# A fused attention and gated-MLP kernel: the U half of w_in by the hardware queue with casts on the engines, and w_spatial and two thirds of batch 1's q transposed by DMA

## The chip, the cores and the metric

One Trainium2 chip, one core. Times are device microseconds of a whole execution. The kernel before took 247.88 us, the median of three runs (247.47, 247.88, 248.72). The profiled execution is the one that took 247.47.

## The reference

Eight batches. Attention with 16 query heads that share 4 key and value heads, over 384 positions of 64 elements, then a gated MLP whose gate mixes positions:

```
k, v repeated 4 times over the heads                 # q: 8 x 16 x 384 x 64; k, v: 8 x 4 x 384 x 64
attn = softmax(q @ k.T / sqrt(64)) @ v
x = attn with the heads side by side                 # 8 x 384 x 1024
h = relu(x @ w_in); u, v = halves of h               # w_in 1024 x 1024, halves of 512
v_n = (v - mean) / sqrt(var + 1e-6)
v_s = w_spatial @ v_n (over positions) + b_spatial   # 384 x 384
out = (u * v_s) @ w_out                              # 512 x 1024
```

Inputs and outputs are fp32. The kernel multiplies in fp16 and sums in fp32.

## The kernel before

All five engines run an order that is written out. Three strings, FIRST (batches 0 to 2 and the weights), STEADY (run for batches 3 to 6) and LAST (batch 7), list steps such as `S,0` or `cq,1,0,0,3,1,0,1,p`; the function `run` calls the function behind each name, and `tc.manual_schedule` keeps that order on every engine and on SP's DMA queue. A step's first number is a batch, relative to the string's; a last letter v, s or p puts a copy or cast on VectorE, ScalarE or GpSimd. An engine takes its own steps strictly in order, so whatever stands behind a step that waits is held too.

The steps that matter here:

- **Loads.** `lk`, `lq`, `lv` load k, q, v of a batch as fp32 by SP's hardware queue (one first q load by ScalarE's). Their fp32 tiles have one buffer, so a batch's load waits for the casts of the batch before. `lwi,0,part,g` (line 249) loads a quarter of one half of w_in by GpSimd's software queue, which casts to fp16 on the way: part 1 is the V half, part 0 the U half, four DMAs each. `lws`, `lbi`, `lwo` load w_spatial, the bias and w_out; w_out comes in four fp32 pieces of 128 rows through two buffers, and `cwo` casts them.
- **Casts and transposes.** `ck`, `cq`, `cv` cast to fp16. For batches 0 and 1 `Tk` and `Tq` transpose on TensorE against an identity (lines 334 and 349), one q tile of four blocks at a time, and `tk`, `tq` copy the PSUM result to SBUF. From batch 2 on, `dk` and `dq` (lines 308 and 317) do it with one DMA transpose each on SP's queue. w_spatial is cast by GpSimd (`cws`, line 274), transposed in nine blocks on TensorE (`Tw`, line 284) and copied by VectorE (`tw`, line 288).
- **Attention.** `S` is one score unit: a pair of matmuls (line 368) into one of two PSUM tiles; a batch has 18, three for each of two head groups and three q tiles. `E` is its exp on ScalarE (line 381), the larger part of ScalarE's work. `X` (line 395) is a third of one q tile's value product; part 2 of it sums the exps. `rl` and `re` make the reciprocal on ScalarE, `rv` on VectorE (line 416, batch 0's first tile only); `xm` multiplies and writes x.
- **MLP.** `V` makes v (line 438), `ru` its relu, `bs`, `rs`, `nm` the normalisation. `G` is a pair of half-array products side by side: `gs` (with w_spatial), `gu` (with the U half of w_in), `go` (with w_out), and `w12`, `w24`, `w10`, which pair `V` of one batch with the output product of another. `mk` is a small write that orders the two phases of a pair. `sa`, `gt` add the bias and gate; `oc` and `st` copy and store the output. LAST uses the unpaired forms `SP`, `U`, `O`.
- **Warm.** `W` are matmuls on the identity that fill TensorE's early waits.

PSUM has two double tiles for scores and four banks that every other product takes in turn; a bank is free again after its last reader.

Of the kernel before, what the change touches and what calls it, by code (L numbers as in the profile page):

```python
# [21 lines left out]
W,0,1 W,0,4 lk,0,0,2 lq,0,0,0,1,0,1,s lq,0,1,0,1 W,0,4 W,0,2 W,0,2 W,0,2 W,0,3 W,0,4 lk,0,2,4  # L22
cq,0,0,0,1,0,0,1,s lq,0,0,1,3 lq,0,1,1,3 lk,1 lv,0 lv,1 lq,1,0 lq,1,1 ck,0,0,0,3,p Tk,0,0,0,3 W,0,4
W,0,4 tk,0,0,0,3,v cq,0,0,0,1,1,0,1,v Tq,0,0,0,0,1 tq,0,0,0,0,1,v W,0,4 ck,0,1,0,3,p
cq,0,1,0,1,1,0,1,p cq,0,1,0,1,0,0,1,p S,0 lk,2 E,0 lws,0 S,0 Tk,0,1,0,3 W,0,4 W,0,2 lq,2,0 lbi,0
Tq,0,1,0,0,1 S,0 lwi,0,1,1 lwi,0,1,2 lwi,0,1,3 cq,0,0,1,3,0,0,1,p tq,0,1,0,0,1,v tk,0,1,0,3,v
cq,0,1,1,3,1,0,1,p cq,0,0,1,3,1,0,1,v W,0,2 E,0 W,0,1 S,0 lq,2,1 E,0 S,0 Tq,0,0,1,0,1 W,0,1 W,0,2
S,0 cq,0,1,1,3,0,0,1,v tq,0,0,1,0,1,v Tq,0,1,1,0,1 S,0 W,0,4 ck,1,1,0,3,p ck,1,0,0,3,p lwi,0,1,0
cv,0,p S,0 W,0,1 Tq,0,1,2,0,1 Tk,1,0,0,3 tk,1,0,0,3,v tq,0,1,1,0,1,v tq,0,1,2,0,1,v Tq,0,0,2,0,1
tq,0,0,2,0,1,v E,0 E,0 E,0 E,0 E,0 S,0 X,0,0,2 S,0 S,0 X,0,0,0 E,0 S,0 rv,0,0 X,0,0,1 xm,0,0,0 E,0  # L30
E,0 S,0 E,0 X,0,1,2 E,0 S,0 xm,0,0,1 X,0,1,1 X,0,1,0 S,0 rl,0,1 E,0 re,0,1 cq,1,0,0,1,0,0,1,p E,0
S,0 Tk,1,1,0,3 V,0,0,0,4 V,0,0,4,8 lwi,0,0,3 S,0 S,0 cq,1,1,1,3,1,0,1,p lwi,0,0,0 lwi,0,0,2 cv,1,v
xm,0,1,1 xm,0,1,0 E,0 ck,2,1,0,3,p cq,1,1,1,3,0,0,1,p cws,0,0 lwi,0,0,1 cq,1,0,1,3,1,0,1,v cws,0,2
cws,0,1 ck,2,0,0,3,p cq,1,0,0,1,1,0,1,s tk,1,1,0,3,v E,0 Tq,1,0,0,0,1 V,0,1,0,4 tq,1,0,0,0,1,v
ru,0,0,v cq,1,0,1,3,0,0,1,v cq,1,1,0,1,0,0,1,v E,0 cq,1,1,0,1,1,0,1,v S,0 X,0,2,2 V,0,1,4,8
Tq,1,1,0,0,1 ru,0,1,v S,0 tq,1,1,0,0,1,v E,0 rl,0,2 S,0 X,0,2,0 re,0,2 E,0 E,0 X,0,2,1 xm,0,2,0
xm,0,2,1 S,0 E,0 Tq,1,0,1,0,1 Tq,1,1,1,0,1 V,0,2,0,4 S,0 S,0 cq,2,0,0,3,1,0,1,p cq,2,0,0,3,0,0,1,p
cq,2,1,0,3,1,0,1,p cq,2,1,0,3,0,0,1,p E,0 E,0 Tw,0,0,2 bs,0,0 tq,1,0,1,0,1,v bs,0,1 tw,0,0,2
tq,1,1,1,0,1,v Tq,1,0,2,0,1 V,0,2,4,8 X,1,0,2 S,0 S,0 ru,0,2,s X,1,0,0 rl,1,0 tq,1,0,2,0,1,v bs,0,2
X,1,0,1 lwo,0,1 dk,2 dq,2,0 lwo,0,0 Tw,0,2,3 Tq,1,1,2,0,1 re,1,0 xm,1,0,0 xm,1,0,1 S,0 E,0 rs,0  # L40
V,1,0,0,4 E,0 tq,1,1,2,0,1,v E,0 nm,0,0 V,1,0,4,8 dq,2,1 tw,0,2,3 nm,0,1 S,0 lwo,0,3 nm,0,2 ru,1,0,v
G,0,gs,2,0,0,1 S,0 lwo,0,2 mk,0,gs,2,v G,0,gs,0,0,0,1 G,0,gs,2,1,0,1 S,0 mk,0,gs,0,v E,0 E,0 E,0
sa,0,2 G,0,gs,0,1,0,1 S,0 sa,0,1 sa,0,0 sa,0,3 bs,1,0 X,1,1,2 E,0 cwo,0,1,1,p rl,1,1 X,1,1,0 X,1,1,1
S,0 cwo,0,0,0,p G,0,gu,2,0,0 S,0 re,1,1 xm,1,1,1 xm,1,1,0 G,0,gu,2,0,1 S,0 cwo,0,0,1,p G,0,gu,0,0,0
E,0 S,0 G,0,gu,0,0,1 mk,0,gu,2,v G,0,gu,2,1,0 lv,2 cwo,0,1,0,v S,0 lq,3,1 lk,3 lq,3,0 mk,0,gu,0,v
E,0 E,0 E,0 G,0,gu,2,1,1 S,0 G,0,gu,0,1,0 S,0 G,0,gu,0,1,1 E,0 S,0 cwo,0,3,1,p cwo,0,2,0,p gt,0,2
gt,0,0 gt,0,1 gt,0,3 cwo,0,3,0,v E,0 cwo,0,2,1,v X,1,2,2 X,1,2,1 S,0 S,0 E,0 E,0 rl,1,2 V,1,1,0,4
re,1,2 E,0 E,0 V,1,1,4,8 S,0 G,0,go,0,0,0 G,0,go,0,0,1 S,0 xm,1,2,1 ru,1,1,v cv,2,p mk,0,go,0,p
X,1,2,0 bs,1,1 xm,1,2,0 E,0 E,0 S,0 G,0,go,0,1,0 S,0 G,0,go,0,1,1 X,2,0,2 X,2,0,0 S,0 E,0 E,0
oc,0,0,v oc,0,1,s rl,2,0 E,0 G,1,w12,2,0,0 re,2,0 G,1,w12,2,0,1 ck,3,0,0,3,s S,0 cq,3,1,0,3,1,0,1,p  # L50
cq,3,1,0,3,0,0,1,p cq,3,0,0,3,1,0,1,p S,0 cq,3,0,0,3,0,0,1,p mk,1,w12,2,v ck,3,1,0,3,v xm,2,0,0 E,0
G,1,w12,2,1,0 G,1,w12,2,1,1 E,0 ru,1,2,s S,0 E,0 dk,3 lk,4 dq,3,0 lv,3 dq,3,1 oc,0,3,v oc,0,2,v S,0
X,2,1,2 rl,2,1 re,2,1 bs,1,2 X,2,0,1 X,2,1,1 E,0 X,2,1,0 S,0 xm,2,0,1 xm,2,1,1 G,2,w24,0,0,0
G,2,w24,0,0,1 S,0 S,0 rs,1 E,0 xm,2,1,0 mk,2,w24,0,v nm,1,0 nm,1,2 nm,1,1 G,2,w24,0,1,0 oc,0,4,v
G,2,w24,0,1,1 E,0 oc,0,5,v E,0 ru,2,0,s S,0 G,1,gs,0,0,0,1 E,0 S,0 mk,1,gs,0,v G,1,gs,0,1,0,1
G,1,gs,2,0,0,1 sa,1,0 mk,1,gs,2,v sa,1,1 S,0 G,1,gs,2,1,0,1 S,0 G,1,gu,0,0,0 sa,1,2 sa,1,3 E,0
G,1,gu,0,0,1 mk,1,gu,0,v S,0 G,1,gu,2,0,0 S,0 G,1,gu,2,0,1 G,1,gu,0,1,0 mk,1,gu,2,v S,0 G,1,gu,2,1,0
G,1,gu,0,1,1 S,0 G,1,gu,2,1,1 E,0 E,0 gt,1,0 gt,1,1 gt,1,2 gt,1,3 E,0 S,0 X,2,2,2 E,0 X,2,2,0 E,0
E,0 rl,2,2 E,0 re,2,2 G,2,w10,1,0,0 G,2,w10,1,0,1 S,0 S,0 mk,2,w10,1,v xm,2,2,0 G,2,w10,1,1,0
oc,1,0,v G,2,w10,1,1,1 S,0 X,2,2,1 oc,1,1,v E,0 E,0 lv,4 st,0,2 lq,4,0 st,0,0 ru,2,1,s cv,3,p bs,2,0  # L60
xm,2,2,1 E,0 lq,4,1 st,1,0 bs,2,1 st,0,1
# [3 lines left out]
cq,1,1,0,3,0,0,1,p X,0,0,2 lk,2 ck,1,1,0,3,p cq,1,1,0,3,1,0,1,p ck,1,0,0,3,p X,0,0,0 S,0 rl,0,0  # L65
G,-1,w12,2,0,0 G,-1,w12,2,0,1 mk,-1,w12,2,v cq,1,0,0,3,1,0,1,p S,0 S,0 re,0,0 E,0 G,-1,w12,2,1,0
G,-1,w12,2,1,1 E,0 xm,0,0,0 cq,1,0,0,3,0,0,1,v oc,-2,2,v S,0 X,0,1,2 dq,1,0 dk,1 lq,2,0 dq,1,1
ru,-1,2,s rl,0,1 oc,-2,3,v re,0,1 X,0,0,1 X,0,1,0 X,0,1,1 bs,-1,2 xm,0,0,1 xm,0,1,0 rs,-1 E,0
G,0,w24,0,0,0 G,0,w24,0,0,1 S,0 S,0 xm,0,1,1 nm,-1,1 mk,0,w24,0,v nm,-1,0 nm,-1,2 E,0 G,0,w24,0,1,0
G,0,w24,0,1,1 oc,-2,4,v S,0 G,-1,gs,0,0,0,1 mk,-1,gs,0,p S,0 E,0 E,0 oc,-2,5,v ru,0,0,s  # L70
G,-1,gs,2,0,0,1 G,-1,gs,0,1,0,1 mk,-1,gs,2,v G,-1,gs,2,1,0,1 S,0 E,0 E,0 sa,-1,0 S,0 X,0,2,2 sa,-1,2
sa,-1,1 sa,-1,3 rl,0,2 X,0,2,0 re,0,2 X,0,2,1 E,0 xm,0,2,0 xm,0,2,1 G,-1,gu,0,0,0 G,-1,gu,0,0,1
mk,-1,gu,0,p S,0 G,-1,gu,2,0,0 G,-1,gu,2,0,1 G,-1,gu,0,1,0 S,0 mk,-1,gu,2,p S,0 bs,0,0 G,-1,gu,0,1,1
gt,-1,0 gt,-1,1 G,-1,gu,2,1,0 G,-1,gu,2,1,1 gt,-1,3 S,0 gt,-1,2 S,0 G,0,w10,1,0,0 G,0,w10,1,0,1 S,0
mk,0,w10,1,v S,0 G,0,w10,1,1,0 oc,-1,0,v G,0,w10,1,1,1 E,0 E,0 E,0 oc,-1,1,v E,0 E,0 S,0 E,0 E,0
lv,2 lq,2,1 E,0 ru,0,1,v E,0 bs,0,1 cv,1,p st,-2,1 st,-1,0 st,-2,2
# [3 lines left out]
S,0 X,0,0,2 G,-1,w12,2,0,0 G,-1,w12,2,0,1 S,0 mk,-1,w12,2,v S,0 G,-1,w12,2,1,0 G,-1,w12,2,1,1 rl,0,0  # L80
E,0 S,0 X,0,0,0 re,0,0 E,0 oc,-2,2,v ru,-1,2,v oc,-2,3,s E,0 bs,-1,2 X,0,1,2 xm,0,0,0 rl,0,1 X,0,0,1
xm,0,0,1 rs,-1 re,0,1 X,0,1,1 X,0,1,0 xm,0,1,1 S,0 G,0,w24,0,0,0 G,0,w24,0,0,1 E,0 E,0 S,0
mk,0,w24,0,v S,0 G,0,w24,0,1,0 E,0 xm,0,1,0 E,0 nm,-1,2 oc,-2,4,v G,0,w24,0,1,1 X,0,2,2 ru,0,0,v
rl,0,2 X,0,2,1 X,0,2,0 re,0,2 V,0,1,0,4 nm,-1,1 V,0,1,4,8 xm,0,2,1 nm,-1,0 xm,0,2,0 ru,0,1,v bs,0,0
SP,-1,1 sa,-1,1 SP,-1,2 V,0,2,0,4 V,0,2,4,8 sa,-1,2 ru,0,2,v oc,-2,5,v bs,0,2 SP,-1,0 SP,-1,3 U,-1,3
bs,0,1 U,-1,1 U,0,0,1 sa,-1,3 gt,-1,1 U,-1,0 U,-1,2 rs,0 nm,0,0 gt,-1,3 nm,0,2 nm,0,1 sa,-1,0 U,0,1
gt,-1,2 gt,-1,0 O,-1,5 O,-1,1 SP,0,1 oc,-1,5,v oc,-1,1,s sa,0,1 st,-2,1 SP,0,3 O,-1,0 SP,0,0 st,-2,2
sa,0,3 gt,0,1 sa,0,0 SP,0,2 O,-1,4 oc,-1,0,v sa,0,2 gt,0,0 oc,-1,4,v O,-1,2 O,-1,3 U,0,2 st,-1,0
st,-1,2 gt,0,2 oc,-1,2,s U,0,3 oc,-1,3,v gt,0,3 O,0,1,0,3 st,-1,1 O,0,4 O,0,1,3,4 O,0,0,0,3
O,0,0,3,4 oc,0,0,s O,0,3 O,0,2 oc,0,4,v oc,0,1,v oc,0,2,s st,0,2,0,512 oc,0,3,v st,0,0  # L90
st,0,1,512,1024 st,0,1,0,512 lo,0,5
# [4 lines left out]
def kernel(  # L96
# [157 lines left out]
    def load_w_out(m):  # L254
        w32 = stage.tile([P, DM], FP32, name=f"w32_{m}", tag="w32", bufs=2)
        nc.sync.dma_start(w32, moe_w_out[m * P : (m + 1) * P, :])
        loaded["w32", m] = w32

    def cast_w_out(m, half, engine):
        cols = slice(half * 512, (half + 1) * 512)  # L260
        copy(w_out16[:, m, cols], loaded["w32", m][:, cols], engine)

    def load_ws():
        ws32 = stage.tile([P, NST, S], FP32, name="ws32", tag="ws32", bufs=1)
        nc.sync.dma_start(ws32, moe_w_spatial.rearrange("(p tt) s -> p tt s", tt=NST))
        loaded["ws32"] = ws32
# [4 lines left out]
    def cast_ws(tt):  # L271
        if tt == 0:
            loaded["ws16"] = stage.tile([P, NST, NST, P], FP16, name="ws16", tag="ws16", bufs=1)
        nc.gpsimd.tensor_copy(
            loaded["ws16"][:, tt, :, :],
            loaded["ws32"][:, tt, :].rearrange("p (s t) -> p t s", t=NST),
        )
# [23 lines left out]
    def behind_w_in(transpose):  # L301

        for g in range(HKV):
            sync(transpose, held["w_in", 0, g])
# [471 lines left out]
```

## Time and profile before

| what | profiled execution |
|---|---|
| its own time | 247.47 us |
| span of the profile | 245.7 us (1.8 us of the time lie outside) |
| TensorE busy | 238.5 us, 97% |
| ScalarE busy | 179.7 us, 73% |
| VectorE busy | 153.1 us, 62% |
| GpSimd busy | 43.9 us, 18% |
| HBM read, written | 25.95 MB, 12.58 MB |
| DMA: hardware queue of SP, software queue of GpSimd | 39.85 MB, 2.10 MB |
| first exp starts | 6.90 us |
| last matmul ends | 241.7 us |

Busy times are sums of what the profiler records for an engine; a matmul's end is modelled, so the idle gaps and the chain of waits say more of TensorE than its busy share. A DMA's row in the profile is its issue; when it landed is seen by who was waiting for it. The 16 DMA engines are shared by all queues, and their busy share can pass 1 since packets overlap. Software loads of w_in are counted with the fp16 bytes that they write.

### The profile page before, as it was taken

How to read it: one execution, taken by the hardware profiler on the slowest of the kernel's cores; microseconds unless marked ns; L12 is line 12 of the kernel's file. 1: busy time of each engine (PE TensorE's matmuls, PEld its weight loads, DVE VectorE, ACT ScalarE, POOL GpSimd, SP SyncE). 2: the span in 40 equal slices, each digit the busy share in tenths (PEclk: the TensorE clock that was granted, in tenths of full speed). 3: DMA queues.
4: the chain of work that ended last, by engine and by line, in shares of the span. 5: the costliest groups of instructions: out<-in, count | busy, mean ns of one | idle time of the engine just before them, and what ended most of it. 6: DMA issues, size and time to landing. Idle time of an engine off the chain costs nothing.

```text
span 245.7 us, 6038 instructions
## 1 busy us (share of the span) xinstructions
PE 238.5 (97%) x2556; PEld 114.8 (47%) x2556; DVE 153.1 (62%) x304; ACT 179.7 (73%) x229; POOL 43.9 (18%) x83
## 2 busy tenths in 40 slices
PE   7899999999999999999999999999999999999993
PEld 6433444534445444554455544554445544455451
DVE  1377778463763478655767368755777346796851
ACT  2899999999997778779697787788697797500111
POOL 1911843134110320013100150011400100000000
PEclk9999999999999999999999999999999999999999
DMA  8999998898789369528990688818690042010056
GB/s 180 292 211 329 275 256 183 186 309 238 148 210 312 114 235 147 148 60 279 246 223 3 187 296 141 183 30 258 204 197 13 0 173 85 4 69 16 31 230 254
DMA packets 57756, 42.73 MB, mean 174 GB/s; under 512 B 26881, under 2 KB 53889, under 8 KB 57729
## 3 DMA queue, kind: packets, MB, share of 16 engines
q1 hardware_dynamic: 54368, 39.85, 58.2%
q0 software_dynamic: 2176, 2.10, 5.3%
q10 hardware_dynamic: 1184, 0.39, 0.6%
q8 instruction: 20, 0.33, 0.6%
q14 instruction: 8, 0.06, 0.1%
HBM read 25.95 MB, written 12.58 MB: 157 GB/s over the span
## 4 chain that ended last, share of the span: by engine, by line
PE 93%; ACT 4%; DMA 1%; issue 0%; DVE 0%; POOL 0%
PE X L395 20%; PE sc L368 13%; PE pu L613 13%; PE po L640 12%; PE pv L600 12%; PE pv L438 5%; PE psp L626 5%; PE po L545 4%; PE pu L510 4%; ACT aT L381 3%; PE psp L484 2%; DMA k<-in_k_dram 1%; PE pq L349 1%; PE sc_u L510 1%; PE po L574 0%
## 5 line engine op out<-in xcount | busy, mean ns | idle before, releaser
L381 ACT ACTIVATE aT<-sc 128x1024 f16<-128x1024 f32 x144 | 139.5, 1023 | 19.7 <-PE sc L368 19.5
L640 PE MATMUL po<-w_out,gT 64*128 64x512 f16 x288 | 66.4, 376 | 0.0
L600 PE MATMUL pv<-w_in,xt 64*128 64x512 f16 x272 | 64.2, 376 | 0.0
L368 PE MATMUL sc<-qT,kT 64*128 64x512 f16 x288 | 49.5, 378 | 1.4 <-ACT aT L381 1.3
L424 DVE TENSOR_TENSOR xt<-X,rec 128x512 f16<-128x512 f32 x48 | 31.7, 684 | 15.8 <-ACT aT L381 6.4
L328 DVE COPY osb<-po 128x512 f32<-128x512 f32 x41 | 28.1, 689 | 14.1 <-PE po L640 8.6
L395 PE MATMUL X<-aT,v 128*32 128x512 f16 x576 | 35.9, 380 | 0.0
L613 PE MATMUL pu<-xt,w_in 64*128 64x384 f16 x384 | 35.2, 323 | 0.0
L640 PEld LDWEIGHTS <-gT 64*128 64x128 f16 x288 | 25.6, 94 | 16.1 <-DVE mark_v L694 3.1
L600 PEld LDWEIGHTS <-xt 64*128 64x128 f16 x272 | 25.1, 94 | 15.8 <-issue 2.5
L328 POOL CAST q<-q 128x768 f16<-128x768 f32 (+2 forms) x27 | 20.6, 775 | 53.3 <-DMA q<-in_q_dram 43.3
L522 DVE SCALAR_TENSOR_TENSOR gT<-pu,v_s 128x384 f16<-128x384 f32 x31 | 16.0, 553 | 18.6 <-PE pu L613 15.9
L368 PEld LDWEIGHTS <-kT 64*128 64x128 f16 x288 | 15.1, 94 | 23.5 <-issue 11.9
L613 PEld LDWEIGHTS <-w_in 64*128 64x128 f16 x384 | 18.4, 94 | 14.9 <-issue 1.7
L496 DVE TENSOR_TENSOR v_s<-psp,bias_b 128x384 f32<-128x384 f32 x32 | 20.4, 687 | 3.8 <-PE psp L626 3.0
L395 PEld LDWEIGHTS <-v 128*32 128x32 f16 x576 | 14.8, 97 | 16.5 <-issue 2.8
L395 PE MATMUL X<-aT,ones 128*32 128x512 f16 x288 | 20.0, 382 | 0.0
L406 ACT ACTIVATE rec<-X 128x512 f32<-128x512 f32 x23 | 13.8, 602 | 8.3 <-PE X L395 8.0
L326 ACT ACTIVATE osb<-po 128x512 f32<-128x512 f32 x6 | 3.6, 598 | 18.6 <-PE po L545 17.6
L459 DVE BATCH_NORM_STATS2 stats<-v_r 128x6 f32<-128x512 f32 x24 | 16.6, 691 | 0.7 <-ACT v_r L451 0.5
L412 ACT ACTIVATE rec<-rec 128x512 f32<-128x512 f32 x23 | 14.5, 630 | 0.6
L470 DVE TENSOR_SCALAR v_n<-v_r,mv,rstd 128x512 f16<-128x512 f32 x24 | 12.3, 539 | 3.9 <-issue 2.7
(56 smaller groups left out, 182.7 us busy)
## 6 DMA issues: line engine op xcount, KB each, us to landing
out_dram<-osb SPq DMA_DIRECT2D x22, 512.0 KB, 3.6
q<-in_q_dram SPq DMA_DIRECT2D x14, 768.0 KB, 7.6
v<-in_v_dram SPq DMA_DIRECT2D x8, 384.0 KB, 3.9
k<-in_k_dram SPq DMA_DIRECT2D x7, 384.0 KB, 4.4
w_in<-in_moe_w_in_dram POOLq DMA_DIRECT2D x8, 256.0 KB, 7.7
w<-in_moe_w_out_dram SPq DMA_DIRECT2D x4, 512.0 KB, 5.0
q<-in_q_dram SPq DMA_DIRECT2D x2, 512.0 KB, 6.4
out_dram<-osb SPq DMA_DIRECT2D x3, 256.0 KB, 2.3
```

Of the source, the lines that this page charges most:

```text
L328: engine.tensor_copy(dst, src)
L368: nc.tensor.matmul(sc[:, half, 0 : 512 // js], kT[b][lo:hi, gp, t, :], qT[b, gp][lo:hi, qt, j0::js], start=True, stop=True,)
L381: nc.scalar.activation(aT[b, qt][:, gp, t].rearrange("p h (j q) -> p h j q", j=G)[:, :, j0::js], held["sc", b, u, j0][:, :, 0 : 512 // js] ...
L395: nc.tensor.matmul(dst[32 * g : 32 * (g + 1), :], v16[:, g, t, 32 * part : 32 * (part + 1)] if part < 2 else ones32, a[:, g // 2, t, g % 2 ...
L412: nc.scalar.activation(r, r, AF.Exp, scale=-1.0)
L424: nc.vector.tensor_tensor(xt[:, jj, :, qt * P : (qt + 1) * P], held["X", b, qt, jj].rearrange("p (j q) -> p j q", j=G), held["rec", b, qt] ...
L459: nc.vector.bn_stats(s6, held["v_r", b, st])
L496: nc.vector.tensor_tensor(held["v_s", b][:, m, :].rearrange("p (t s) -> p t s", t=NST), held["psp", b, m][:, 0:S].rearrange("p (t s) -> p ...
L522: nc.vector.scalar_tensor_tensor(held["gT", b][:, mu, :], held["pu", b, mu][:, 0:S], 0.0, held["v_s", b][:, mu, :], op0=ALU.max, op1=ALU.mult,
L600: yield lambda kc=kc: nc.tensor.matmul(held["pv", b, st], xT[b][rows, kc, st * P : (st + 1) * P], w_in16[rows, kc, DH:DFF], start=(first a ...
L613: yield lambda kc=kc: nc.tensor.matmul(held["pu", b, mu][:, 0:S], w_in16[rows, kc, mu * P : (mu + 1) * P], xT[b][rows, kc, :], start=(firs ...
L640: yield lambda m=m: nc.tensor.matmul(held["po", b, i], held["gT", b][rows, m, tt * P : (tt + 1) * P], w_out16[rows, m, half * 512 : (half ...
```

## The change

Four things change together.

1. The U half of w_in no longer comes by GpSimd's software queue. `lwu,0,i,g` loads it as fp32 by SP's queue, eight DMAs of 256 KB, into a ring of two buffers of 8 KB per partition (tag `w32`), and eight steps `cwu` cast one slice of 128 x 512 each: five on GpSimd, two on VectorE, one on ScalarE.
2. The ring also takes w_spatial's fp32 (the first of its five uses) and w_out, which now comes in two DMAs of 1 MB. The fp16 copy of w_spatial uses an output buffer's space.
3. w_spatial is transposed by one DMA (`dw`, nine blocks), and q tiles 1 and 2 of batch 1 by two DMAs (`dqt`, eight blocks each). The 9 + 16 TensorE transposes and their six PSUM copies go. These DMAs are held until the software loads of the V half have landed.
4. The written order of all three strings is another one. Among other things, v of batch 0 is SP's first load, ahead of k; k's first cast and PSUM copy move to ScalarE; the first value product comes after eight score units, where it came after nine; v of batch 1 is loaded behind half of U; and the loads and transposes stand on SP's queue thus: `lwu` x8 with `lbi`, `lv,1`, `dqt`, `dqt`, `dw` among them, `lq,2,0 lq,2,1 lwo,0,0 dk,2 dq,2,0 dq,2,1 lwo,0,1 lv,2 lq,3,0 lq,3,1 lk,3`. Some relus, casts and output copies change engines.

The cores of it (FIRST's head, of the three strings):

```diff
-W,0,1 W,0,4 lk,0,0,2 lq,0,0,0,1,0,1,s lq,0,1,0,1 W,0,4 W,0,2 W,0,2 W,0,2 W,0,3 W,0,4 lk,0,2,4
+lv,0 lk,0,0,2 lq,0,1,0,1 W,0,4 lq,0,0,0,1,0,1,s ck,0,0,0,3,s W,0,4 W,0,4 W,0,2 W,0,2 W,0,4 W,0,2
...
+    def load_w_u(i, g):
+        if ("w32", i) not in loaded:
+            loaded["w32", i] = stage.tile([P, 4, DH], FP32, name=f"w32_{i}", tag="w32", bufs=2)
+        r0 = (g * 8 + i * 4) * 32
+        nc.sync.dma_start(
+            loaded["w32", i][32 * g : 32 * (g + 1), :, :],
+            moe_w_in[r0 : r0 + 128, 0:DH].rearrange("(kc r) n -> r kc n", r=32),
+        )
+    def cast_w_u(kc, engine):
+        copy(w_in16[:, kc, 0:DH], loaded["w32", kc // 4][:, kc % 4, :], engine)
-    def load_w_out(m):
-        w32 = stage.tile([P, DM], FP32, name=f"w32_{m}", tag="w32", bufs=2)
-        nc.sync.dma_start(w32, moe_w_out[m * P : (m + 1) * P, :])
+    def load_w_out(mp):
+        w32 = stage.tile([P, 4, DH], FP32, name=f"w32_{2 + mp}", tag="w32", bufs=2)
+        nc.sync.dma_start(
+            w32.rearrange("p (m h) n -> p m (h n)", m=2),
+            moe_w_out[2 * mp * P : 2 * (mp + 1) * P, :].rearrange("(m p) n -> p m n", p=P),
+        )
...
+    def dma_transpose_ws():
+        behind_w_in(
+            nc.sync.dma_start_transpose(
+                wsT16.rearrange("p s (t q) -> p (s t) q", t=NST),
+                loaded["ws16"].rearrange("p s t q -> p (s t q)"),
+            )
+        )
...
     def behind_w_in(transpose):
         for g in range(HKV):
-            sync(transpose, held["w_in", 0, g])
+            sync(transpose, held["w_in", 1, g])
...
-    def dma_transpose_q(b, gp):
-        new_qT(b, gp)
+    def dma_transpose_q(b, gp, t0=0, t1=NST):
+        if (b, gp) not in qT:
+            new_qT(b, gp)
         transpose = nc.sync.dma_start_transpose(
-            qT[b, gp].rearrange("p t j q -> p (t j) q"),
-            loaded["q16", b, gp].rearrange("p t j h d -> p (t j h d)"),
+            qT[b, gp][:, t0:t1].rearrange("p t j q -> p (t j) q"),
+            loaded["q16", b, gp][:, t0:t1].rearrange("p t j h d -> p (t j h d)"),
         )
-        if b == 2:
+        if b <= 2:
             behind_w_in(transpose)
```

## The prediction

> **What bounds the kernel now.** I read the page first (busy shares and slices), then the chain of waits in order of time, then windows by stage, the DMA view of short windows, and last the timeline around the changed steps.
>
> The page: TensorE is busy in nearly every slice, and the DMA row is nearly full for the first third.
>
> ```profile
> span 245.7 us, 6038 instructions
> PE 238.5 (97%) x2556; PEld 114.8 (47%) x2556; DVE 153.1 (62%) x304; ACT 179.7 (73%) x229; POOL 43.9 (18%) x83
> PE   7899999999999999999999999999999999999993
> DMA  8999998898789369528990688818690042010056
> ```
>
> The chain of waits (start, length, what) has three parts. Until 6.9 us it waits for k; until 15.3 us it is ScalarE's exps, nine at 0.93 us each; from there to the last store it is TensorE with no gap above half a microsecond. The pieces that the change takes out stand in that last part:
>
> ```profile
> 0.75 2.74 DMA k<-in_k_dram
> 3.54 0.51 POOL k L328
> 6.90 8.37 ACT aT L381 x9
> ...
> 29.18 0.55 PE pq L349 x8
> 31.13 0.61 PE psw L284 x6
> 31.74 0.22 PE pq L349 x4
> ...
> 35.54 0.27 PE psw L284 x3
> 35.81 0.22 PE pq L349 x4
> ```
>
> So what leaves TensorE after 15 us is gained in full, if its inputs still come in time. The windows by stage (busy time and count per engine, TensorE clock, DMA share, GB/s) show what else is full in the stage that the change touches: ScalarE to 97%, and the DMA engines over 100%, since packets overlap.
>
> ```profile
> 20.00:30.00 10.00, 10.00 (x98) 4.21 (x91) 7.31 (x15) 9.68 (x13) 5.52 (x10) 1.00 1.11 304
> 30.00:40.00 10.00, 10.00 (x100) 4.34 (x100) 7.61 (x20) 8.54 (x13) 3.68 (x6) 1.00 1.02 247
> ```
>
> The DMA view of three short windows gives prices: plain loads of 768-byte rows (19 to 24 us), software loads alone, counted in fp16 bytes (12 to 15 us), and DMA transposes (45.6 to 47.4 us).
>
> ```profile
> DMA packets 2157, 1.63 MB, mean 326 GB/s; under 512 B 32, under 2 KB 2157, under 8 KB 2157
> DMA packets 623, 0.61 MB, mean 202 GB/s; under 512 B 32, under 2 KB 623, under 8 KB 623
> DMA packets 1560, 0.43 MB, mean 238 GB/s; under 512 B 1550, under 2 KB 1550, under 8 KB 1560
> ```
>
> The timeline shows how near the transfers are to their users. Batch 2's second q load releases its cast at 39.59; the last w_out piece releases its cast at 53.45, and the output product that reads it starts its first half at 54.19 and its second, the one that needs that piece, at 54.62.
>
> ```profile
> 39.59 1.60 POOL L328 CAST q<-q 128x768 f16<-128x768 f32 x2 [3.60 <-DMA q<-in_q_dram]
> 53.45 0.43 DVE L328 CAST w_out<-w 128x512 f16<-128x512 f32 x1 [0.98 <-DMA w<-in_moe_w_out_dram]
> 54.19 1.03 PE L640 MATMUL po<-w_out,gT 64*128 64x512 f16 x8
> ```
>
> **What leaves TensorE.** 16 q transposes and 9 w_spatial transposes: the five pieces above, 1.87 us. Start to start they cost a little less (1.7), as the 0.1 us at a change of operand shape stays in part (the chain has score pairs at 0.22 and, at such a change, at 0.32). I take -1.8. The rest of TensorE's list after the first value product is the same work in another order; warm matmuls are 51 in both. Their six PSUM copies on VectorE (0.35 to 0.56 each) go too; VectorE is at 76% there, so that is worth nothing.
>
> **The head.** SP's first issue becomes v of batch 0 (393 kB, 1.2 us at 326 GB/s), with k behind it. k landed at 3.49. If only v's own time is added it lands at 4.7; if it also waits for all of the q load that ScalarE's queue issues at the same moment (262 kB, 1.1 us at 238) at 5.8. Then ScalarE casts k (0.51), three transposes start (0.3) and q's may follow: 5.6 to 6.7, against 5.35 in the timeline now. I take the nearer to the top, since the ACT queue's q is already in front of SP's second load today: first exp +0.9 (0.25 to 1.35). ScalarE paces the head, so this is paid in full.
>
> Two smaller waits come behind it. The exps keep 0.93, but the eleventh is now wanted by a score pair placed earlier; and the 3.36 us reciprocal on VectorE, now behind a k cast (0.55) and ahead of the copy of batch 1's k, holds PSUM banks that the next transposes and value products need. Together 0.2 to 0.6; I take 0.4. Without any DMA trouble the sum is -1.8 + 0.9 + 0.4 = -0.5.
>
> **What is added to the DMA engines.** The U half of w_in: eight loads of 262 kB at 326 are 6.4 us, where the software loads took 8 x 1.3 for both halves, 5.2 for this one: +1.2. Three transposes: 8, 8 and 9 blocks of 128 rows of 256 B, 819 kB, 3.4 us at 238; at the pace of the first k transpose (197 kB between 39.5 and 41.0, 131 GB/s) 6.3. I take 3.5, as a stream behind a full queue resembles the 238 row. So +4.7 us in a stage where the queue has no idle time before 47.4.
>
> [...]
>
> **Where it becomes late.** SP's queue is in order: behind q of batch 2 stands half of w_out (now 1 MB in one DMA, 3.2 us), which waits for VectorE's cast of a U slice, and only behind it k's and q's transposes for batch 2, then the other half of w_out. Ahead of batch 2's first q transpose, from 10.3 us (batch 0's loads end at 9.1 now, plus v): k 1.2, V half 5.2, q 4.8, w_spatial 1.8, k 1.2, U half 6.4, bias 0.6, v 1.2, transposes 3.5, q 4.8, w_out 3.2, k transpose 0.8, q transpose 1.65: 36.4. The same prices applied to the kernel before give 27.2 from 9.1 to the end of q of batch 2, 36.9 with 0.6 for landing (an estimate: the first k transpose's packets end near 41.0, and issued at 38.36 it lands, by the 3.1 of its tile's view, near 41.5); the cast there was released at 39.6. So prices are 3% short (with the w_out piece that mixed in) to 9%. After: it lands between 48.3 and 50.5. The first score of batch 2 reads it; with no stall its place is 48.3 (48.1 now, -0.5, +0.65 for one quarter of the U product that now stands ahead). Stall 0 to 2.2.
>
> The last w_out half: 36.4 + 1.65 + 3.2 = 41.2, so it lands at 53.3 to 55.8, and GpSimd casts two pieces (0.61 to 0.87 each) beside VectorE's two: 54.5 to 57.5. Its user's place is 54.1 (54.62 - 0.5). Stall 0.3 to 3.3. By the other route, today's 53.4 plus 4.7 less the queue's idle 1.1 near 48 gives 57.0, with casts 58.2: 4.1. The delays do not add: the later one counts. I take 2.2, inside both. Behind TensorE in that wait stand scores, so ScalarE runs dry too.
>
> Between these, GpSimd's cast of the fifth U slice stands behind the casts of batch 2's q, done near 43.5 where the U product wants it at 43.7; inside the same sum. U's casts (0.6 each on GpSimd, ScalarE, VectorE) displace what GpSimd has room for; ScalarE's one cast, and two w_out casts later, cost up to 0.5 where it is full, hidden by the stall.
>
> Sum: -0.5 + 2.2 = +1.7 on the profiled execution's own 247.47 (span 245.7), which was the lowest of three with median 247.88: 249.2. About 0.5% is what a measurement of this kernel can tell from no change.
>
> **Rivals.** *TensorE stays fed (faster).* If the queue runs at the 326 row without the 3 to 9%, as fewer software packets are mixed in, q of batch 2 lands by 47.5 and w_out by 53, and only the head counts: -1.8 + 0.3 to 0.9 + 0.2, so 246.2 to 247.0, and 245.8 with no head delay. It decides at 48.3 and 54.1. For it: transfers were never awaited by TensorE after 15 us so far. Against it: the last w_out piece had 0.7 us left, and 4.7 us are added. *Queue much later.* Transposes at 131 GB/s, and w_out held by its ring: stall 4 to 6, 251 to 253. *The head alone pays*: the k delay at 1.35 and the stall under 1: 247.5 to 248.5.
>
> **How the numbers follow.** Stall of 1.7 to 4 (my forecast): 0.42, 248.7 to 251; much later: 0.13; head and small stall, near no change: 0.25; fed: 0.20, of which most passes the 0.5% mark. Range 246.3 to 252.3. Faster 0.17, same 0.30, slower 0.53.
>
> **What would show it.** Right: TensorE's waits in the window 40 to 60 name a cast of w_out, a cast of w_in or a DMA into qT; first exp near 7.8. Wrong: no gap on TensorE from 15 to 60 us and the span shorter by the five pieces; or gaps before 40 us (w_spatial or batch 1's q transposed late); or gaps in the later batches, whose order also changed and which I count as equal work.

## The result and the profile after

The kernel after takes 254.16 us, the median of four runs (253.51 to 254.95); the kernel before took 247.70 beside it. The ratio is 1.0254 (95% interval 1.0213 to 1.0295): 6.5 us slower, where 1.7 slower was forecast and 252.3 was the upper end of the range. The profiled execution is one of 254.14.

The page after (span, busy times, the slices of TensorE and of the DMA engines) shows TensorE no longer at 9 in nearly every slice. It has 25 instructions fewer to do (2531 for 2556) and yet is spread over a longer span, and the dips lie in the first quarter.

```profile
span 252.4 us, 6020 instructions
PE 239.8 (95%) x2531; PEld 114.6 (45%) x2531; DVE 152.4 (60%) x306; ACT 184.0 (73%) x233; POOL 41.9 (17%) x75
PE   6889989779999999999999999999999999999993
DMA  7999999999799209890499309970692012100066
```

The chain of waits up to 62 us (start, length, what). Before, it was TensorE alone from 15.3 us on. Now transfers and casts stand in it: k at the head, q of batch 1, GpSimd's cast of batch 1's v, and 9.87 us of w_out.

```profile
1.27 4.66 DMA k<-in_k_dram
5.96 0.53 ACT k L355
...
13.79 12.10 DMA q<-in_q_dram
...
34.87 0.84 POOL v L357
35.74 0.83 PE X L424 x12
...
41.73 9.87 DMA w<-in_moe_w_out_dram
51.62 0.63 ACT w_out L355
52.25 1.82 ACT aT L410 x2
```

The windows by stage (busy time and count of PE, PEld, DVE, ACT, POOL, then TensorE clock, DMA share, GB/s): TensorE, which was busy for 10.00 of 10 in these stages, loses 1.2 to 1.6 us in each, and the DMA engines have hardly any room left (0.96 to 1.25). First the two rows of the kernel before from 40 us on, then the three of the kernel after:

```profile
40.00:50.00 10.00, 10.00 (x130) 5.17 (x124) 5.71 (x12) 9.59 (x12) 2.92 (x5) 1.00 0.86 184
50.00:60.00 10.00, 10.00 (x110) 3.71 (x108) 5.80 (x11) 9.85 (x13) 4.18 (x6) 1.00 0.99 306
```

```profile
30.00:40.00 10.00, 8.78 (x78) 3.05 (x77) 7.19 (x15) 8.68 (x14) 1.55 (x3) 1.00 1.25 218
40.00:50.00 10.00, 8.54 (x106) 4.17 (x106) 5.53 (x11) 7.51 (x9) 4.95 (x8) 1.00 1.23 306
50.00:60.00 10.00, 8.45 (x86) 3.72 (x82) 4.56 (x11) 8.34 (x11) 1.45 (x4) 1.00 0.96 261
```

The timeline names the three waits in full (start, length, engine, line, operation, in square brackets the idle time before it and what ended it).

```profile
35.74 0.83 PE L424 MATMUL X<-aT,v 128*32 128x512 f16 x12 [1.22 <-POOL v L357]
...
45.81 1.60 POOL L357 CAST q<-q 128x768 f16<-128x768 f32 x2 [1.29 <-PE sc L397]
47.35 0.61 POOL L357 CAST w_in<-w 128x512 f16<-128x512 f32 x1
48.02 0.82 PE L642 MATMUL pu<-xt,w_in 64*128 64x384 f16 x8 [1.47 <-POOL w_in L357]
...
51.62 0.63 ACT L355 ACTIVATE w_out<-w 128x512 f16<-128x512 f32 x1 [3.96 <-DMA w<-in_moe_w_out_dram]
52.16 1.92 ACT L410 ACTIVATE aT<-sc 128x1024 f16<-128x1024 f32 x2
53.22 0.39 PE L397 MATMUL sc<-qT,kT 64*128 64x512 f16 x2 [1.12 <-ACT aT L410]
```

In order: the value product stands for v's cast, as v landed at 34.81; the U product stands for the cast of the fifth slice, which stands behind two casts of batch 2's q on GpSimd; and ScalarE stands 3.96 us at its cast of w_out, with the exps queued behind it, so TensorE gets no score tile back.

**Where the 6.8 us went.** The last matmul ends at 241.65 before and at 248.46 after. I took the start-to-start time of each TensorE step in both traces and subtracted what the same step usually costs (a score pair 0.22, a third of a value product 0.65, and 0.1 more at a change of operand shape: the chain has score pairs at 0.32 and thirds of a value product at 0.76 there). TensorE's own list is 1.4 us shorter. Up to the first value product 1.3 is lost. From there on 7.6 is lost after, against 0.7 before. The 6.9 between them: 0.8 at the 12th and 13th score pairs, 1.4 at batch 1's v, 1.6 at the fifth slice, 2.1 around ScalarE's wait, 0.3 at the second half of w_out, 0.6 at the w_spatial products of batch 1 near 77 us, and 0.1 in crumbs. -1.4 + 1.3 + 6.9 = 6.8.

About half of the 1.3 belongs to this one execution. TensorE's granted clock was 0.50 in it from 8.48 to 11.90 us, where the kernel before had 1.00. In the traces of t_back and u128 below, which have the same head and no such stretch, the first value product starts at 14.14, against 14.82 here. Two other executions of the kernel after, with a mean clock of 1.00, took 253.51 and 254.19, so the stretch doesn't show in the time.

### The profile page after: what moved, and what is told of

Read it like the earlier page. It is cut to its first block, busy times and chain, and to the rows that moved or that the text cites. A ratio compares the mean times of both kernels' runs of the same rounds, so it can differ in the third digit from the quotient of the medians.

```text
span 252.4 us, 6020 instructions
## 1 busy us (share of the span) xinstructions
PE 239.8 (95%) x2531; PEld 114.6 (45%) x2531; DVE 152.4 (60%) x306; ACT 184.0 (73%) x233; POOL 41.9 (17%) x75
## 4 chain that ended last, share of the span: by engine, by line
PE 75%; DMA 11%; ACT 6%; issue 2%; DVE 2%; POOL 2%; SPq 1%; POOLq 0%
PE X L424 15%; PE pv L629 11%; PE po L669 11%; PE pu L642 10%; PE sc L397 10%; DMA q<-in_q_dram 5%; ACT aT L410 4%; DMA w<-in_moe_w_out_dram 4%; PE po L574 4%; PE psp L655 4%; PE pu L539 4%; PE pv L467 2%; DMA k<-in_k_dram 2%; PE psp L513 2%; POOL osb_ws L294 1%
## 5 line engine op out<-in xcount | busy, mean ns | idle before, releaser
L397 PE MATMUL sc<-qT,kT 64*128 64x512 f16 x288 | 51.4, 382 | 3.2 <-ACT aT L410 2.2
L424 PE MATMUL X<-aT,v 128*32 128x512 f16 x576 | 36.6, 380 | 1.2 <-POOL v L357 1.2
L642 PE MATMUL pu<-xt,w_in 64*128 64x384 f16 x384 | 35.9, 323 | 1.5 <-POOL w_in L357 1.5
L669 PEld LDWEIGHTS <-gT 64*128 64x128 f16 x288 | 26.4, 94 | 15.4 <-DVE mark_v L723 2.6
L357 DVE COPY osb<-po 128x512 f32<-128x512 f32 x33 | 22.6, 687 | 16.5 <-PE po L669 8.1
L357 POOL CAST q<-q 128x768 f16<-128x768 f32 (+2 forms) x31 | 22.4, 753 | 29.2 <-DMA q<-in_q_dram 27.9
L355 ACT ACTIVATE osb<-po 128x512 f32<-128x512 f32 x14 | 8.4, 598 | 18.2 <-PE po L574 17.5
L723 DVE MEMSET mark_v<- 1x1 f32 x32 | 1.9, 59 | 28.9 <-PE pu L642 16.4
```

What stands on the lines that cost most here:

```text
L357: engine.tensor_copy(dst, src)
L397: nc.tensor.matmul(sc[:, half, 0 : 512 // js], kT[b][lo:hi, gp, t, :], qT[b, gp][lo:hi, qt, j0::js], start=True, stop=True,)
L424: nc.tensor.matmul(dst[32 * g : 32 * (g + 1), :], v16[:, g, t, 32 * part : 32 * (part + 1)] if part < 2 else ones32, a[:, g // 2, t, g % 2 ...
L642: yield lambda kc=kc: nc.tensor.matmul(held["pu", b, mu][:, 0:S], w_in16[rows, kc, mu * P : (mu + 1) * P], xT[b][rows, kc, :], start=(firs ...
L669: yield lambda m=m: nc.tensor.matmul(held["po", b, i], held["gT", b][rows, m, tt * P : (tt + 1) * P], w_out16[rows, m, half * 512 : (half ...
```

## The experiments

The theory that came out of the two traces: SP's queue and the DMA engines are behind nearly all the way from 20 to 55 us (*the backlog*; the DMA share in the trace of after is 1.15 over this stretch, and in quarters of a microsecond it is under 0.6 only from 33.75 to 34.75, from 50.0 to 51.25 and in the last one), mainly as the eight U loads are slower than they were priced. The rivals: the written order itself is bad, or single steps stand in the wrong place and *each delay adds*. All runs but the last four change the kernel after; those change the kernel before. Each row is the median of four or five runs with the ratio to the kernel before in the same session.

| run | us | ratio to before | 95% interval |
|---|---|---|---|
| after | 254.16 | 1.0254 | 1.0213 to 1.0295 |
| order_only | 254.69 | 1.0245 | 1.0207 to 1.0282 |
| t_back | 255.01 | 1.0299 | 1.0240 to 1.0359 |
| act_free | 255.55 | 1.0286 | 1.0250 to 1.0323 |
| act_late | 255.28 | 1.0294 | 1.0258 to 1.0329 |
| v0 | 253.29 | 1.0203 | 1.0157 to 1.0248 |
| order_fix | 253.58 | 1.0229 | 1.0197 to 1.0262 |
| u_sw | 254.81 | 1.0245 | 1.0189 to 1.0300 |
| u128 | 254.17 | 1.0235 | 1.0206 to 1.0263 |
| u128p | 251.64 | 1.0149 | 1.0115 to 1.0183 |
| u128p_v0 | 251.43 | 1.0158 | 1.0114 to 1.0202 |
| u128v | 269.10 | 1.0837 | 1.0787 to 1.0887 |
| u128v_v0 | 268.13 | 1.0793 | 1.0747 to 1.0840 |
| b_v0 | 250.55 | 1.0077 | 1.0051 to 1.0103 |
| b_uhw | 250.58 | 1.0088 | 1.0058 to 1.0118 |
| b_all | 254.66 | 1.0259 | 1.0223 to 1.0295 |
| b_all_u128 | 252.01 | 1.0139 | 1.0115 to 1.0163 |

### One mechanism taken back, the order kept

**order_only**: both mechanisms of before in the order of after.

```diff
-lwu x8, cwu x8, dqt,1,0,1,3 dqt,1,1,1,3 dw,0
+lwi,0,0,0 lwi,0,0,1 lwi,0,0,2 lwi,0,0,3
+Tq,1,0,1,0,1 Tq,1,1,1,0,1 Tw,0,0,2 Tq,1,0,2,0,1 Tw,0,2,3 Tq,1,1,2,0,1 (each with its copy)
```

> The kernel after's written order with both mechanisms of the kernel before: U half of w_in by GpSimd's software queue without cast steps, all 25 blocks transposed on TensorE. Theory 'late data' (the loads by the hardware queue and the transposes by DMA fill SP's queue, and what stands behind them is late): only the head (+1.2) and some 0.5 to 1 in the later batches are left of the loss, so 249.0 to 250.0, with no wait of TensorE over 0.5 us between 30 and 60 us. Rival 'order' (the written order puts steps where they hold their engine whatever the loads do): 252 to 254.

254.69: nearer to the rival's 252 to 254, and 0.7 above it. But the losses are new ones: TensorE stood 1.0 us for a cast of batch 1's q, behind software load issues on GpSimd, and 1.15 for a multiply on VectorE that stood behind the PSUM copies of the transposes. In the profiled execution that wait was followed by 3.4 us at half clock (shown at the end); another execution, with a mean clock of 1.00, took 254.98, so this stretch doesn't explain the time. The order was written for the new mechanisms, so this run doesn't separate order from mechanism.

**t_back**: the 25 blocks back on TensorE, U still by the hardware queue.

```diff
-dqt,1,0,1,3 dqt,1,1,1,3 dw,0
+Tq,1,0,1,0,1 Tq,1,1,1,0,1 Tw,0,0,2 Tq,1,0,2,0,1 Tw,0,2,3 Tq,1,1,2,0,1 (each with its copy)
```

> The kernel after with the 16 q blocks and 9 w_spatial blocks back on TensorE, U half still by the hardware queue. Theory 'the U loads are the late data': TensorE gets 1.8 us of work back, the queue is 3.5 us shorter behind batch 1's v, so w_out lands near 48 and ScalarE's wait for it goes (-2), but the waits for batch 1's v (1.4) and for the fifth U slice (up to 1.6) stay: 253 to 254.5. Rival 'the DMA transposes are the late data': 250 to 251.5, with batch 1's v in time.

255.01, with an interval that overlaps that of after. TensorE's list is 1.4 us longer again, and the last matmul ends at 248.34 in its trace, against 248.46: between these two traces, the saved TensorE work was spent waiting. The medians are 0.9 apart, so that a part of it reached the end can't be excluded. The waits that were expected to stay are nearly gone (0.3 for v, none for the fifth slice). In their place TensorE stood 1.4 us behind a multiply on VectorE, 1.1 and 0.5 ahead of k's transposes, and 0.6 for batch 2's q transpose. The queue did gain room: batch 2's two q loads landed at 42.67 and 45.71, against 45.66 and 48.88 in after, although v ahead of them landed 0.65 later, so the three transposes had cost the queue an estimated 3.6 to 3.9 us. That room passed unused. The first w_out half landed at 50.47, not near 48: it was issued only at 45.06, when VectorE's late cast of a U slice had freed the ring's buffer, and between 44 and 46 us the DMA share was 0.06.

**u_sw**: the U half by the software queue, the transposes still by DMA.

```diff
-lwu x8, cwu x8
+lwi,0,0,3 lwi,0,0,0 lwi,0,0,2 lwi,0,0,1 (behind the first cws)
-            sync(transpose, held["w_in", 1, g])
+            sync(transpose, held["w_in", 0, g])
```

> The kernel after with the U half of w_in again by GpSimd's software queue (four loads with cast, issued behind the first w_spatial cast), no U casts on the engines, and the 25 blocks still transposed by DMA; w_out's two loads then find their buffers free at once. Theory 'the U loads by the hardware queue are the cost': some 4 us of DMA time and eight casts less, batch 1's v and the U half in time, w_out near 47: no TensorE wait over 0.7 us from 30 to 60 us, 249 to 250.5 (the head's 1.2 and some 0.5 later stay, the 1.8 of transposes is won). Rival 'the order itself': 252 or more, with waits elsewhere.

254.81, the rival's number for another reason. The DMA transposes are held until the last software load has landed (36.16), so batch 1's q tiles landed at 39.54, and the score waited 2.4 us for them. From 33.5 to 37.5 us the DMA share was 0.12, so the engines stood idle under that gate and this run doesn't test the pace of the U loads. Software loads of U and early DMA transposes exclude each other under that gate. U by the hardware queue is what lets the transposes go early.

### Steps moved out of the waits

```diff
act_free:  -cwo,0,1,0,s cwo,0,1,1,s   +cwo,0,1,0,p cwo,0,1,1,p
act_late:  cwo,0,1,0,s and cwo,0,1,1,s behind V,1,1,0,4, at the end of batch 1
v0:        lv,0 behind lk,0,2,4; cv,0,v behind tk,0,1,0,3,v
order_fix: v0; lv,1 ahead of lwu x8; cwu,0,4,p ahead of cq,2,0,...; act_late
```

> The kernel after with the two w_out casts on ScalarE given to GpSimd; nothing else is changed. Theory 'ScalarE held by one cast' (it waits 4.0 us for w_out while exps stand behind it): TensorE's waits from 50 to 55 us go, 2.0 to 2.3 us less, 252.0. Rival 'backlog of the DMA queue' (the next late thing, k and q transposes of batch 2 that land at 52.3 and 53.5, takes its place): 253.3 to 254.

> The kernel after with ScalarE's two w_out casts put later in the written order, just ahead of the last value products of batch 1; nothing else is changed. Theory 'the cast holds the exps' (ScalarE waits 4.0 us for w_out with exps queued behind that cast): TensorE's waits from 50 to 56 us (0.2, 1.3, 0.6) go, 252.0 to 252.6. Rival 'the backlog': the first score of batch 2 then stands for its q transpose, which lands at 53.5 where it would be wanted near 51.8, 253.5 to 254.2.

255.55 and 255.28: no gain, against the theory that the held cast by itself costs 2 us. ScalarE no longer stands for w_out, and the next late transfer takes its place, as the rival said. The three longest waits of TensorE in act_late from 44 to 64 us (an exp and a small write on GpSimd end two more, of 0.4 and 0.2):

```profile
PE pu L642 <- POOL w_in L357: 1.5, 1, 1.5
PE po L669 <- POOL w_out L357: 0.7, 2, 0.4
PE sc L397 <- DMA qT<-q: 0.7, 1, 0.7
```

Both came out about 1 us above after, which neither theory has. The intervals overlap, and the profiled executions differ from that of after ahead of the steps that were moved: in act_late batch 1's v landed at 35.64 (34.81), in act_free the first value product started at 16.20 (14.82). What the 1 us is stays open.

> The kernel after with v of batch 0 loaded behind all of k of batch 0 and cast later on VectorE; nothing else is changed. The first exp should start near 7.0 in place of 8.1. Theory 'delays add': the head's 1.2 us come off the end, 252.9 to 253.2. Theory 'one backlog' (what sets the end is when w_out lands, and the DMA queue's work ahead of it is the same): TensorE only waits longer behind, 253.9 to 254.4.

253.29: 0.9 less than after, close to the theory that delays add, though the two intervals overlap. The first exp started at 7.51 (7.0 was expected) and the lead was used up by the ninth (15.90, against 16.14 in after, and 15.62 to 15.68 in t_back and u128, which have the head of after). What stayed is on the queue: GpSimd's first software load was issued 1.2 us earlier (6.33, 7.54), the loads behind it landed earlier too, most of them by up to 1.6, v of batch 1 at 33.21 in place of 34.81, and the wait for it went. The head moves the backlog too, which I had put into neither theory.

> The kernel after with four moves in the written order and no other change: v of batch 0 behind k, v of batch 1 ahead of the U loads, GpSimd's cast of the fifth U slice ahead of its casts of batch 2's q, and ScalarE's two w_out casts later. Theory 'delays add': 1.0 + 1.4 + 1.6 + 1.5 off, 248.5 to 249.5. Rival 'the backlog' (the DMA queue's work ahead of batch 2's first q transpose is the same, so TensorE arrives early and waits there): 251.5 to 253.

253.58, where delays that add would have given 248.5 to 249.5. The waits for v and for the fifth slice are gone, and TensorE stands 1.2 us for a small GpSimd write behind casts of batch 2's q (landed at 47.19) and 0.7 for the q transpose. Four moves at four places bring no more than the first of them alone: the later data set the end, not the places. The rival's range (251.5 to 253) was still too low.

### The pace of the U loads

A load of `lwu` writes 32 partitions, four slices each. **u128** brings the same bytes in the same packets of 2 KB to all 128 partitions, from contiguous rows.

```diff
-            loaded["w32", i][32 * g : 32 * (g + 1), :, :],
-            moe_w_in[r0 : r0 + 128, 0:DH].rearrange("(kc r) n -> r kc n", r=32),
+            loaded["w32", i][:, g, :], moe_w_in[r0 : r0 + 128, 0:DH],     # r0 = (4 * i + g) * 128
```

> The kernel after with each of the eight U loads writing all 128 partitions (rows of w_in in another place, so the U half's values are wrong) instead of 32; same bytes and packets of 2 KB. Theory 'the 32 partitions slow the load': eight loads take 6.4 us in place of 9.6, batch 1's v lands 1 to 1.5 us earlier and all behind 3 us earlier, 251.5 to 252.5. Rival 'the rate is that of the queue, whatever the destination': loads stay near 1.2 us each, 253.8 to 254.5.

The DMA view of a stretch with little but U loads: first in the kernel after (29.0 to 30.3 us), then in u128p below (26.6 to 27.6 us).

```profile
DMA packets 166, 0.30 MB, mean 228 GB/s; under 512 B 18, under 2 KB 25, under 8 KB 166
```

```profile
DMA packets 209, 0.38 MB, mean 383 GB/s; under 512 B 21, under 2 KB 25, under 8 KB 209
```

So 262 kB take 1.15 us onto 32 partitions and 0.69 onto 128: 9.2 against 5.5 us for the eight, where the prediction had 6.4. The 3.7 us between the two shapes are shown; the order in which the rows are read changes with the partitions, and no run separates the two. The time didn't move (254.17): batch 1's v and the fifth slice came in time, and one wait of 2.4 us behind ScalarE's w_out cast took the place of both. The reason was not the DMA engines, which were at 0.32 between 44 and 46 us. The ring had dealt w_out the other buffer, whose last reader is the late cast of the fifth slice on GpSimd: SP waited 4.6 us for that cast, issued w_out at 44.66, and it landed at 50.11. **u128p** deals the buffers as the kernel after has them.

```diff
-tag="w32", bufs=2
+tag="w32_b", bufs=1     # w32_0, w32_2; "w32_a" for w_spatial, w32_1, w32_3
```

> The earlier run with U loads onto all 128 partitions from contiguous rows (the U half's values are wrong), now with the ring's two buffers dealt as in the kernel after: there w_out had been given the buffer of the slices that GpSimd casts last, and was issued at 44.7 although the DMA engines were idle. Theory: w_out is issued near 41 and lands by 48, ScalarE's wait falls from 4.0 to under 1 and the first q transpose of batch 2 lands by 50: 249.8 to 251. Rival: some other wait holds the stretch, 253 or more.

251.64, with the interval below that of after: 2.5 us. w_out was issued at 40.39 and landed at 47.95, the q transpose at 50.01, as expected; ScalarE's wait fell from 4.0 to 1.6, not under 1. The range was missed by 0.6.

> The run before it with v of batch 0 behind k (the U half's values are wrong here too). If both the head and the DMA backlog are off the path, what is left of the loss is the later batches' 0.6 and a few tenths at the 12th score: 248.5 to 249.8. If 251 or more, a part of the loss is neither.

251.43, no different from u128p. By its own criterion, part of the loss is neither the head nor the pace of U; the last four runs narrow it down.

Two runs tried the same with the right rows, a slice of w_in per load, in four groups of 32 rows.

```diff
+        rows = moe_w_in[:, 0:DH].rearrange("(g kc r) n -> kc g r n", g=4, r=32)
+        nc.sync.dma_start(loaded["w32", i][:, g, :], rows[i * 4 + g])
```

> The kernel after with the same U rows, but each of the eight loads brings one slice of 128 x 512 to all 128 partitions in place of four slices to 32 of them, and the ring's two buffers are dealt by hand as in the kernel after. Theory 'the slow 32-partition loads': the loads pass in 0.7 us each, w_out lands at 47 to 48.5, the waits for batch 1's v (1.4) and the fifth slice (1.6) go and ScalarE's 4.0 us wait falls under 1: 249.3 to 250.5. Rival 'it forms again': some engine's order holds w_out or its casts as before, 253 or more.

> The run before it and the late v of batch 0 together. Theory: with the backlog gone the head's delay is no longer hidden, so it comes off in full: 1.0 to 1.2 below the run with the 128-partition loads alone, 248.2 to 249.4, level with the kernel before or 0.5% above. Rival: nothing gained over either alone.

269.10 and 268.13: all theories missed. The window 34.0 to 36.5 us of u128v, in the columns of the stages above, has a DMA share of 0.26 at 98 GB/s: an estimated 4.2 of the 16 engines at work.

```profile
34.00:36.50 2.50, 1.36 (x15) 0.41 (x13) 1.57 (x3) 2.44 (x4) 0.00 (x0) 1.00 0.26 98
```

These loads write all 128 partitions, as those of u128p do, which ran at 383 GB/s. What differs is the source: four groups of 32 rows here, so that its outer dimension is 4, and 128 contiguous rows there. Why this one is so much slower, no run shows.

### Single parts in the order of the kernel before

**b_v0** only moves `lv,0` to the front of the kernel before. **b_uhw** brings U by the hardware queue in it, with all eight casts on GpSimd and w_out in two loads; **b_all** adds the DMA transposes; **b_all_u128** adds the loads of u128p.

```diff
b_v0:  -lk,0,0,2 ... lk,1 lv,0     +lv,0 lk,0,0,2 ... lk,1
b_uhw: -lwi,0,0,0 ... lwi,0,0,3    +lws,0 lk,2 lwu x4 lbi,0 lwu x4 lq,2,0 lq,2,1, and cwu,0,0,p to cwu,0,7,p ahead of cq,2
b_all: -Tw, Tq,1 of tiles 1 and 2  +dqt,1,0,1,3 dqt,1,1,1,3 dw,0 among the last four lwu, as in the kernel after
```

> The kernel before with one move: v of batch 0 is SP's first load, ahead of k. Theory (the head is paid in full, since ScalarE paces it and nothing behind waits for data): k lands 2.4 us later and the first exp 1.0 later, 248.5 to 249.2. Rival (the head is given back at a later wait): 247.6 to 248.2.

250.55, 1.0077 (1.0051 to 1.0103): 1.9 us and more than expected. The first exp started at 9.80 in place of 6.90. k landed at 6.19, where it landed at 3.49: that is 2.7 of the 2.9. The rest is a slower first score pair (0.61 us, against 0.39 before). From k's landing to the first exp 3.6 us pass here and 3.4 in the kernel before, but 2.2 in after (5.94 to 8.11).

> The kernel before's order and TensorE transposes, with the U half of w_in by the hardware queue in eight loads of 32 partitions, all eight casts on GpSimd, and w_out in two loads through the same ring. Theory (the U loads at their measured 1.2 us each make the queue some 4.4 us longer, and batch 2's q and w_out late): a stall at the first score of batch 2 or at the first output product, 249.5 to 252. Rival (before's order has room for it): 247.7 to 248.5.

250.58, 1.0088: 2.2 us, inside the range. The theory's two stalls are there, and TensorE has hardly another wait from 30 to 62 us:

```profile
PE po L671 <- POOL w_out L359: 1.5, 1, 1.5
PE sc L399 <- DMA qT<-q: 1.1, 1, 1.1
```

These stalls are not the pace of the loads alone. The ring's first use is w_spatial, so the fifth U load was issued only at 32.67, behind GpSimd's casts of w_spatial (30.66 to 32.64), and from 31.75 to 34.0 us the DMA share was 0.20 at 47 GB/s: an estimated 1.8 us of the DMA engines unused. And w_out's first 1 MB stands ahead of batch 2's q transpose, where 0.5 MB stood. The 2.2 us are U by the hardware queue with its ring and the larger w_out load; no run takes these apart.

> The run before it with the 25 blocks of w_spatial and batch 1's q transposed by DMA too: both mechanisms of the change in the order of the kernel before, with k ahead of v of batch 0. Theory (DMA backlog): 1.8 us less TensorE work, but 3.5 us more on the queue, so the stall grows by as much or more: 250 to 253. Rival (the written order was the cost): 246.5 to 248.

254.66, 1.0259: as slow as the kernel after, with k ahead of v and the order of before. 4.1 us lie between b_all and b_uhw, although TensorE has 25 blocks less to do. The same view of b_all has one line that matters, and its timeline shows what follows the longer of the two waits:

```profile
PE sc L397 <- DMA qT<-q: 5.3, 2, 4.1
```

```profile
53.08 0.61 PE L397 MATMUL sc<-qT,kT 64*128 64x512 f16 x2 [4.13 <-DMA qT<-q]
53.45 1.51 PE L642 MATMUL pu<-xt,w_in 64*128 64x384 f16 x8
```

Batch 2's first q transpose landed at 52.94, against 50.64 in b_uhw. These 2.3 us are less than the three transposes cost, as in b_all they also fill time that b_uhw leaves unused (the DMA share from 30 to 36 us is 1.19, against 0.69). (The other of the two waits, 1.2, is for batch 1's q transpose.) After the wait eight half-array products take 1.51 us, where they took 0.81 ahead of it, as the window of 52 to 58 us has a granted clock of 0.50 to 0.54. That costs 2.3 more by the sum of the steps. All four executions of b_all have a mean clock of 0.98 to 0.99, so each of them had some of it.

> The run before it with each U load onto all 128 partitions from contiguous rows (the U half's values are wrong), which took 0.7 us in place of 1.2. Theory (the pace of the U loads decides the trade): 3 to 4 us less backlog, 246.5 to 248.5, level with the kernel before or faster. Rival: no better than the run before it.

252.01, 1.0139: 2.7 us less than b_all, so the shape of the U loads, which u128p changes, is that part of the loss on this order too. It is not all: a wait of 2.8 for the q transpose stays, and the range (to 248.5) was missed. With three transposes on the queue the trade loses 3.5 us even with fast U loads.

## Why the prediction was wrong

The sign, the first exp, the in-order queue (from 51.56 us on SP issues `dq`, `lwo`, `lv`, `lq`, `lk` as written, the last at 56.62) and the two data that come late (batch 2's q and w_out) were as forecast. The size was off by a factor of four, 6.5 for 1.7. By its steps:

- **What leaves TensorE, -1.8.** The list is 1.4 shorter. With the 25 blocks back in t_back the last matmul ends no later (248.34 against 248.46), so in these traces none of it reached the end; the two medians, 0.9 apart, leave a part of it open.
- **The head, +0.9.** The first exp came 1.2 later, inside the 0.25 to 1.35 given. b_v0 shows that the same move alone costs 1.9 in the order of before. The written order of after takes back a part of it (2.2 us from k's landing to the first exp, against 3.6 in b_v0); which of its steps does so, k's cast on ScalarE or the warm matmuls, isn't separated.
- **Two smaller waits, +0.4.** 0.8 at the 12th and 13th score pairs.
- **The U loads, 6.4 us at 326 GB/s.** This is the first step that failed, a mis-sized term: 9.2 at 228. The price was read from a stretch of loads onto 128 partitions, and no row of before showed a hardware load onto 32. The traces show 228 GB/s onto 32 partitions (after) against 383 onto 128 (u128p). u128p takes 2.5 us of the loss away, and b_all_u128 2.7; their loads, at 5.5 us for the eight, are faster than the 6.4 that was priced.
- **The transposes, 3.5 us.** By t_back they cost the queue an estimated 3.6 to 3.9, near the price. From b_uhw to b_all the landing of q goes back by 2.3 only (50.64 to 52.94), as a part of them fills time that b_uhw left unused. But they fell into a backlog that was already past its limit, so what they added was stall. With the slowed TensorE behind that stall, b_all is 4.1 slower than b_uhw.
- **The landing of batch 2's first q transpose, 48.3 to 50.5.** 53.54, 3.0 beyond the range: 2.8 of it is what the U loads took above their price. The prediction also read before's queue as without idle time up to 47.4; its DMA share is 0.35 from 38.25 to 39.75 us and 0.24 from 40.75 to 41.5. That overlooked some 1.5 us of room, an error to the other side. The last w_out half landed at 59.06, not at 53.3 to 55.8.
- **Where w_out is wanted.** This is the second step that failed. I set the demand at its user, the output product at 54.1, and called ScalarE's two w_out casts worth "up to 0.5 ..., hidden by the stall". ScalarE came to the first of them at 47.67 and stood there 3.96 us with the exps behind it. Yet act_late, which moves only those casts, brings nothing: with them away, q's transpose and the casts of w_out stall in their place. So this decides where the backlog is paid and not how much.
- **Batch 1's v and the fifth U slice.** v's new place behind half of U was in the list, and its user at 34.5 was not checked: 1.4. The cast of the fifth slice I had "done near 43.5 where the U product wants it at 43.7"; it was done at 47.96, as batch 2's q in front of it landed at 45.66.
- **"The delays do not add".** Right in structure, as u128 shows, where two waits fell away and the time stayed. The last of them was 5.4 late (1.4 + 1.6 + 2.1 + 0.3), not 2.2.
- **Later batches as equal work.** 0.6 is lost near 77 us in every run with the strings of after, and not in those with the strings of before: this part belongs to the written order.

The rival *queue much later* had the nearest number, 251 to 253, still under the 254.16, with another mechanism (transposes at 131 GB/s, and w_out held by its ring). The ring's hold is there, 2.4 us up to the issue of w_out's first half at 41.73, but the DMA engines were full in that time (a share of 1.10 from 39.30 to 41.73). What of the loss in the kernel after is order and what is mechanism can't be given as a sum: the parts measured one by one on the order of before (1.9 for v first, 2.2 for U with its ring, 4.1 for the transposes with the slow clock behind them) make 8.2, more than the 6.5 of all together.

## What to carry to other kernels

Price a new transfer by its own shape: 262 kB took 1.15 us onto 32 partitions and 0.69 onto 128, loads whose source had an outer dimension of 4 ran at 98 GB/s, and the rate read off another load was 43% too high here (326 for 228). A wait for data counts from the first instruction on any engine that touches the data, the cast included (ScalarE stood 3.96 us at its cast), and from all that is queued behind it. If moving that instruction only moves the wait, as in act_late (255.28, no gain on 254.16), the queue is the bound, and what helped here was faster loads: 2.5 us in u128p, 2.7 in b_all_u128. Before blaming the bytes, see whether the queue is full at that time: a buffer ring that two loads share can hold the queue while the DMA engines stand idle, as in t_back (a share of 0.06), u128 (0.32) and b_uhw (0.20).

## What the runs showed of the hardware

- Hardware loads of 262 kB ran at 228 GB/s onto 32 partitions (after) and at 383 onto 128 (u128p), with the same 2 KB packets; those whose source had an outer dimension of 4 (u128v) ran at 98 GB/s with a DMA share of 0.26.
- A wait of TensorE cost twice in b_all: the clock was at 0.50 from 51.02 us, within a wait of 4.1 us, to 57.85, 4.8 us behind its end, and the steps in it took 2.3 us more. Shorter waits were followed by it or not: after 2.85 us in b_all_u128 and 2.42 in u_sw a stretch of 3.4 us at 0.50 followed, after 2.44 in u128 none did; and order_only and t_back both stood 1.15 us at the same product near 40 us, and the seven matmuls behind took 3.14 us in the one and 1.68 in the other. What decides stays open. The two timelines, order_only first:

```profile
41.02 0.39 PE L467 MATMUL pv<-w_in,xt 128*128 128x512 f16 x1 [1.15 <-DVE xt L453]
41.61 3.14 PE L467 MATMUL pv<-w_in,xt 128*128 128x512 f16 x7 [0.21 <-DVE xt L453]
```

```profile
40.75 0.39 PE L468 MATMUL pv<-w_in,xt 128*128 128x512 f16 x1 [1.15 <-DVE xt L454]
41.35 1.68 PE L468 MATMUL pv<-w_in,xt 128*128 128x512 f16 x7 [0.21 <-DVE xt L454]
```
